# Transposing a gathered block by a DRAM round trip and VectorE's 32x32 blocks instead of on TensorE, in a routed MoE kernel

## The chip, the cores and the metric

The kernel runs on one core of a Trainium2 chip. The metric is the time on the device in microseconds (us), the median of several runs. The profile is one further execution, taken with the hardware profiler.

## The reference

Attention in chunks of 32 positions over 4 x 8 heads comes first; its output, 3072 tokens of 512 numbers, goes through a mixture of 8 experts, of which each token takes the one with the highest logit:

```
x = attn_out.transpose(0, 2, 1, 3).reshape(3072, 512)
logits = x @ w_gate + modality_bias[modality_id]
e_idx = argmax(logits, axis=1)
gate_w = softmax(logits)[arange(3072), e_idx]
for e in range(8):
    mask = e_idx == e
    h = maximum(x[mask] @ w1[e], 0)          # 512 -> 1024
    out[mask] = gate_w[mask, None] * (h @ w2[e])   # 1024 -> 512
```

All arrays are float32.

## The kernel before, in words

The first 160 us or so compute the attention and the routing. The attention output lies in DRAM as `xd`, one row of 512 numbers and the gate for each token; tables on the chip list for each expert its tokens.

The rest is a row of **slots**. A slot multiplies 256 tokens of one expert. `slot(row)` does three things at once: TensorE multiplies the tokens that the slot before prepared, the queues fetch the tokens and weights of `row`, and ScalarE and VectorE prepare them. The rows in this execution are 0 (in the first part of the program), 1, 2, 3, then 12 and 13 (`ROW_R1`, `ROW_X`), 14 to 17 (four of seven optional ones) and 33, 34; the last slot has no row to prepare. Eight optional short slots between 3 and 12 are skipped. The text calls the slot that prepares row 12 "slot 12".

A slot has two phases on TensorE. The first is `mm1(f)` for f = 0 to 7, 12 matmuls each: a product of float32 numbers is made of three products of rounded parts, the high part of w by the high and low part of x (`xth`, `xtl`), and the low part of w by the high part of x. The second is `mm2(f)`, 6 matmuls each. In the first phase ScalarE and VectorE finish h and split the eight blocks of w2 into parts (`conv(8 + f)`: a cast on ScalarE, a subtraction on VectorE). In the second they split the eight blocks of w1 of the next row (`conv(0)` to `conv(7)`, in `prepare(f)`), and TensorE transposes the next row's x: `trans(half)`, twice four 128x128 transposes into PSUM, from where ScalarE and VectorE take the two parts. Slots 3 and 12 also bring 32 extra tokens each (`gather_rest`, `trans_rest`), which the slot behind multiplies along.

SyncE (SP) issues the weight loads, in program order: w1 of a row at the head of its slot, w2 behind the first phase, eight transfers of 256 KB each. From row 1 on a load has a condition, which is false where the expert is that of the row before; then nothing is moved. GpSimd (POOL) issues the indirect transfers in its program order: the store of the results, then `keep` (it copies the lists and gates that the store and `finish` need later), then the gather of the next 256 tokens. SP, POOL, TensorE and, in this part, ScalarE and VectorE run in the order in which the program is written. Each optional slot is a branch on every engine; at the end of a skipped group the engines pass a join, where each one waits for its own work and then counts its semaphores on.

Of the kernel before, what the change touches and what calls it, by code (L numbers as in the profile page):

```python
# [20 lines left out]
P = 128  # L21
# [12 lines left out]
HEAD = 3  # L34
LAST = 3
# [17 lines left out]
def tile_chunk_attention_top1_moe(  # L53
# [31 lines left out]
    xd = dram.tile([N, XW], F32, name="xd")  # L85
    qf = q.rearrange("b h s d -> (b h s) d")
# [588 lines left out]
    w1h, w1l = [xa.tile([P, 8, 512], F32R, name=f"w1{i}") for i in range(2)]  # L675
    for f in range(8):
        raw[f] = xa.tile([P, 512], F32, name=f"raw{f}")
        wh[f], wl[f] = w1h[:, f], w1l[:, f]
    xp = hp = xg = xth = xtl = ix = gx = hh = hl = None
    ix_now = const.tile([P, 2], I32, name="ix_now")  # L680
    gate_now = const.tile([P, 2], F32, name="gate_now")
    ev = {}

    def load_w(row, half):
        if half == 0:
            if row == 0:
                ev[0] = nc.values_load(regs0[0:1, 0:1], engines=[mybir.EngineType.SP], min_val=0, max_val=E - 1,
                                       skip_runtime_bounds_check_because="the place of one of 8 experts")
            else:
                r = (regs1 if row < 2 else regs)[row:row + 1]  # L690
                ev[row] = nc.values_load(r[:, 0:1], engines=[mybir.EngineType.SP], min_val=0, max_val=E - 1,
                                         skip_runtime_bounds_check_because="the place of one of 8 experts, or 0")
                ev[row, "c"] = nc.values_load(r[:, 1:2], engines=[mybir.EngineType.SP], min_val=0, max_val=1,
                                              skip_runtime_bounds_check_because="a comparison gives 0 or 1")
        e = ev[row]
        kw = {} if row == 0 else {"cond": ev[row, "c"]}
        for f in range(8):
            if half == 0:
                nc.sync.dma_start(
                    raw[f].rearrange("p (c f) -> p c f", f=P),  # L700
                    w1[ds(e, 1), :, f * P:(f + 1) * P].rearrange("o (c p) f -> p (o c) f", p=P), **kw)
            else:
                nc.sync.dma_start(raw[8 + f], w2[ds(e, 1), f * P:(f + 1) * P, :].rearrange("o p d -> p (o d)"), **kw)
# [31 lines left out]

    def trans(half):
        t = bank().rearrange("p (c n) -> p c n", c=2)
        for cc in range(2):
            for tt in range(2):
                c = 2 * half + cc  # L740
                nc.tensor.transpose(t[:, cc, tt * P:(tt + 1) * P], xg[tt][:, c * P:(c + 1) * P], ident)  # L741
        sl = slice(2 * half, 2 * half + 2)
        nc.scalar.copy(xth[:, sl, 0:256], t)  # L743
        nc.vector.tensor_sub(xtl[:, sl, 0:256], t, xth[:, sl, 0:256].bitcast(F32))

    def trans_rest(i):
        t = bank()[:, 0:4 * NR].rearrange("p (c n) -> p c n", c=4)
        for c in range(4):
            nc.tensor.transpose(t[:, c], xgr[i][:, c * P:(c + 1) * P], ident[0:NR, 0:NR])
        nc.scalar.copy(xth[:, :, 256:], t)  # L750
        nc.vector.tensor_sub(xtl[:, :, 256:], t, xth[:, :, 256:].bitcast(F32))

    def mm1(f, rest=False):
# [36 lines left out]
    def finish(t):  # L790
        nc.scalar.activation(outs[t], pos[t], AF.Copy, scale=gate_now[:, t:t + 1])  # L791

    def store():
        put = [
            nc.gpsimd.indirect_dma_start(  # L795
                out=out, out_offset=bass.IndirectOffsetOnAxis(ap=ix_now[:, t:t + 1], axis=0), in_=outs[t], in_offset=None,
# [151 lines left out]
    gxr = hp.tile([NR, 1], I32, name="gxr")  # L948
    outs = [hp.tile([P, DM], F32, name=f"o{t}") for t in range(2)]
# [19 lines left out]
    def begin(row, opening=False):  # L969
        if row is not None:  # L970
            load_w(row, 0)
        if not opening:
            for t in range(2):
                finish(t)
            store()
        keep()
        if row is not None:
            gather(row)

    def prepare(f):  # L980
        for i in ((0, 1), (2, 3), (4,), (5,), (6, 7))[f] if f < 5 else ():
            conv(i)
        if f in (2, 3):
            trans(f - 2)

    def slot(row, rest=None, rest_next=None, opening=False):
        begin(row, opening)
        if rest_next is not None:
            gather_rest(rest_next)
        if not opening:  # L990
            for f in range(8):
                mm1(f, rest is not None)
                conv(8 + f)
        if rest is None and row is not None:
            load_w(row, 1)
        for f in range(6):
# [10 lines left out]
            elif row is not None:  # L1007
                prepare(f)
            if f == 3 and rest_next is not None:
                trans_rest(rest_next)  # L1010
        mm2(6, (0,))
        mm2(7, (0,))
        if row is None:
            finish(0)
# [9 lines left out]
        if row is None:  # L1024
            finish(1)
            store()
# [71 lines left out]
```

## Time and profile before

| | |
|---|---|
| median of 3 runs | 453.59 us (453.19 to 454.4) |
| profiled execution | 455.18 us, its span 453.4 us |
| TensorE matmul | 425.5 us busy, 94% of the span |
| VectorE | 310.5 us, 68% |
| ScalarE | 261.6 us, 58% |
| GpSimd | 195.8 us, 43% |
| DMA | 61.66 MB, mean 136 GB/s |

Busy time is what an engine's instructions took, and the share is that of the whole span, the attention part included. Matmuls overlap, so the start of one to the start of the next tells more than the duration of one.

### The profile page before, as it was taken

What the parts mean: (1) busy time and instruction counts of PE and PEld (TensorE: products, weight loads), DVE (VectorE), ACT (ScalarE), POOL (GpSimd) and SP (SyncE); (2) the same over time, 40 slices, a digit from 0 to 9 for tenths busy, and PEclk for the clock granted to TensorE, in tenths of its full rate; (3) what the DMA queues carried; (4) which work ended last, traced back from release to release, by engine and by line L of the source; (5) the groups of instructions that cost most, each with busy time, mean ns of one, the idle gap of its engine ahead of it and who ended that gap; (6) DMA issues with size and microseconds to landing.
All of it is one profiled execution on the core that took longest, in us unless ns stands there. A gap on an engine that the chain in (4) does not pass through costs nothing. (4 is left out here: it accounts for less than half of the span.)

```text
span 453.4 us, 11700 instructions
## 1 busy us (share of the span) xinstructions
PE 425.5 (94%) x4009; PEld 359.0 (79%) x4009; DVE 310.5 (68%) x746; ACT 261.6 (58%) x524; POOL 195.8 (43%) x373
## 2 busy tenths in 40 slices
PE   7879999999977998999999999999999999999993
PEld 4658787776856787989796977989898988898982
DVE  7888799797877699848465454757666574848430
ACT  5747776675636664747366455656565655657421
POOL 8867679579798932214051211303040404040201
PEclk9989999999979999999999999999999999999997
DMA  6899999999977502177196834202662201111101
GB/s 185 149 227 205 220 218 205 207 209 198 220 180 213 192 3 93 54 227 226 38 261 208 225 97 142 90 0 95 180 210 76 90 5 50 47 49 48 46 2 46
DMA packets 74818, 61.66 MB, mean 136 GB/s; under 512 B 36091, under 2 KB 64979, under 8 KB 74740
## 3 DMA queue, kind: packets, MB, share of 16 engines
q1 hardware_dynamic: 68000, 41.50, 40.2%
q0 software_dynamic: 5888, 19.11, 13.8%
q8 instruction: 36, 0.59, 0.6%
q14 instruction: 42, 0.34, 0.3%
q10 hardware_dynamic: 852, 0.11, 0.2%
HBM read 77.43 MB, written 12.76 MB: 199 GB/s over the span
## 5 line engine op out<-in xcount | busy, mean ns | idle before, releaser
L760 PEld LDWEIGHTS tr<-xt,w 128*128 128x128 f32 x1152 | 141.0, 189 | 4.9 <-issue 2.6
L760 PE MATMUL tr<-xt,w 128*128 128x256 f32 (+1 forms) x1152 | 142.9, 284 | 1.8 <-PEq L1059 0.6
L770 PE MATMUL av<-wh,h 128*128 128x512 f32 x384 | 128.4, 400 | 0.0
L795 POOL DMA_INDIRECT out_dram<-o,ix_now x24 | 24.2, 1008 | 157.1 <-ACT o L791 156.2
L764 DVE SCALAR_TENSOR_TENSOR h<-tr,h 128x256 fp32r<-128x256 f32 x96 | 40.6, 423 | 70.8 <-ACT h L761 53.1
L770 PEld LDWEIGHTS av<-wh,h 128*128 128x128 f32 x384 | 72.2, 188 | 17.3 <-issue 1.7
L770 PE MATMUL av<-wl,h 128*128 128x512 f32 x192 | 75.8, 395 | 0.0
L289 POOL COPY vw<-vw 24x384 f32<-24x384 f32 (+1 forms) x128 | 61.1, 515 | 24.5 <-DMA vw<-in_v_dram 23.2
L708 DVE TENSOR_TENSOR wl<-raw,wh 128x512 fp32r<-128x512 f32 x91 | 63.0, 692 | 8.1 <-ACT wh L706 0.8
L761 ACT ACTIVATE h<-tr 128x256 fp32r<-128x256 f32 x96 | 36.8, 385 | 51.8 <-PE tr L760 32.7
L708 DVE TENSOR_TENSOR w<-raw,w 128x512 fp32r<-128x512 f32 x93 | 60.4, 694 | 8.4 <-ACT w L706 8.4
L706 ACT CAST wh<-raw 128x512 fp32r<-128x512 f32 x96 | 58.8, 614 | 1.3 <-DMA raw<-in_moe_w_dram 1.3
L706 ACT CAST w<-raw 128x512 fp32r<-128x512 f32 x96 | 53.8, 622 | 0.0
L791 ACT ACTIVATE o<-av,gate_now 128x512 f32<-128x512 f32 x24 | 16.2, 689 | 46.3 <-PE av L770 37.3
L770 PEld LDWEIGHTS av<-wl,h 128*128 128x128 f32 x192 | 36.2, 188 | 7.1
L331 ACT COPY kbd<-tr 64x672 f32<-64x672 f32 x47 | 36.5, 777 | 6.4 <-PE tr L325 5.5
L369 PE MATMUL av<-vw,PT 128*32 128x130 f32 x768 | 29.3, 286 | 3.7 <-ACT PT L359 1.8
L359 ACT ACTIVATE PT<-tr 128x384 f32<-128x384 f32 x32 | 15.8, 492 | 28.6 <-PE tr L357 28.1
L339 PE MATMUL sc<-kbd,qT 128*32 128x128 f32 x768 | 29.3, 289 | 1.9 <-POOL kbd L313 1.9
L723 POOL DMA_INDIRECT xg<-xd,gx x24 | 26.5, 1105 | 9.8 <-POOL gx L721 6.2
L369 PEld LDWEIGHTS av<-vw,PT 128*32 128x32 f32 x768 | 20.5, 113 | 9.3 <-ACT PT L359 4.3
L743 ACT CAST xt<-tr 128x512 fp32r<-128x512 f32 x24 | 13.9, 586 | 23.0 <-PE tr L741 13.4
(237 smaller groups left out, 524.5 us busy)
## 6 DMA issues: line engine op xcount, KB each, us to landing
raw<-in_moe_w_dram SPq DMA_DIRECT2D x192, 256.0 KB
k<-in_k_dram SPq DMA_DIRECT2D x16, 384.0 KB
q<-in_q_dram SPq DMA_DIRECT2D x16, 384.0 KB
xd<-xb POOLq DMA_DIRECT2D x16, 384.0 KB, 6.0
vw<-in_v_dram SPq DMA_DIRECT2D x32, 184.0 KB
vw<-in_mem_v_dram SPq DMA_DIRECT2D x32, 48.0 KB
vw<-in_v_dram SPq DMA_DIRECT2D x32, 6.0 KB
vw<-in_v_dram SPq DMA_DIRECT2D x32, 2.0 KB
```

What stands on the lines that cost most here:

```text
L289: nc.gpsimd.tensor_copy(vw[r0:r0 + 24, c + 1:c + 1 + w, h, 0:D], vw[r0 + 32:r0 + 56, c:c + w, h, 0:D])
L331: copy(dst.rearrange("p c (i j) -> p c i j", j=2)[:, :, :, j], win)
L339: nc.tensor.matmul(sc[32 * j:32 * j + 32, t * P:(t + 1) * P], qT[:, 32 * c:32 * c + 32], kbd[:, c].rearrange("p h m -> p (h m)"), start=Tr ...
L369: nc.tensor.matmul(avb[32 * j:32 * j + 32, t * W:(t + 1) * W], PT[:, t * P + 32 * j:t * P + 32 * j + 32], vw[:, c].rearrange("p h d -> p ( ...
L706: nc.scalar.copy(wh[i], raw[i])
L708: (eng or nc.vector).tensor_sub(wl[i][:, s], raw[i][:, s], wh[i][:, s].bitcast(F32))
L723: nc.gpsimd.indirect_dma_start(out=xg[t], out_offset=None, in_=xd[0:rows], in_offset=bass.IndirectOffsetOnAxis(ap=gx[:, t:t + 1], axis=0))
L760: nc.tensor.matmul(pw, wt[f][:, c * P:(c + 1) * P], x[:, c, 0:w], start=(n == 0), stop=(n == 11))
L761: nc.scalar.activation(hh[:, f], ph, AF.Relu)
L764: nc.vector.scalar_tensor_tensor(hl[:, f], ph, 0.0, hh[:, f].bitcast(F32), op0=ALU.max, op1=ALU.subtract)
L770: nc.tensor.matmul(pos[t], x, w[8 + f], start=(f == 0 and n == 0), stop=(f == 7 and n == 2))
L795: nc.gpsimd.indirect_dma_start(out=out, out_offset=bass.IndirectOffsetOnAxis(ap=ix_now[:, t:t + 1], axis=0), in_=outs[t], in_offset=None, ...
```

## The change

From row 3 on (`NWHOLE` = 3) x is no longer transposed by TensorE. `send` copies the gathered rows to DRAM (`xs`, and `xsr` for the 32 extra tokens), and `fetch` reads them back as `xq`: partition 32a + s holds quarter a (128 of the 512 numbers) of the tokens s, 32 + s, 64 + s and so on. VectorE transposes 32x32 blocks of it (`turn`, and `turn_rest` for the extra tokens) into `xv`, and `turned` splits `xv` into its two parts as before. Rows of x then stand in another order over the partitions, so w1 is loaded in that order too: each of the eight transfers now fills 32 partitions with four pieces of 512 numbers (2 KB) where before each filled 128 partitions with four pieces of 128 (512 bytes), and a block of w1 is complete only when four transfers have landed. Row 3 loads w1 without a condition. Send and fetch stand in SP's order in front of the w1 load.

On POOL, `keep` and the gather now stand in front of the store, in every slot; the list and the gates that the store and `finish` still need are copied once more (`ix_out`, `gate_out`).

SP at the head of slot 3, before (`raw_2957` is the last block of w2 of row 2, `raw_188` and `raw_189` the first blocks of w1 of row 3):

```order
L703 DMA raw_2957<-in_moe_w_dram 128x512
L691 TENSOR_LOAD regs
L693 TENSOR_LOAD regs
L699 ISA
L699 DMA raw_188<-in_moe_w_dram 128x4x128
L699 ISA
L699 DMA raw_189<-in_moe_w_dram 128x4x128
```

The same place now (`raw_2955` is the last block of w2 of row 2, `raw` is w1):

```order
L713 DMA raw_2955<-in_moe_w_dram 128x512
L755 DMA xsr_85<-xgr_2958 32x512
L757 DMA xs<-xg_2709 128x512
L757 DMA xs<-xg_2710 128x512
L763 DMA xqr<-xsr_85 32x128
L764 DMA xq<-xs 32x8x128
...
L695 TENSOR_LOAD regs
L697 TENSOR_LOAD regs
L709 ISA
L709 DMA raw<-in_moe_w_dram 32x4x512
```

Three sends and eight fetches (four pairs) stand between the last w2 block and the first w1 transfer; in slots without extra tokens there are two sends and four fetches.

VectorE in the second phase of slot 3, before (`w` is the low part of w1, `xt` that of x):

```order
L708 TENSOR_TENSOR w_187<-raw_191,w_186 128x512
L708 TENSOR_TENSOR w_187<-raw_192,w_186 128x512
L744 TENSOR_TENSOR xt_2714<-tr,xt_2713 128x2x256
L708 TENSOR_TENSOR w_187<-raw_193,w_186 128x512
L744 TENSOR_TENSOR xt_2714<-tr,xt_2713 128x2x256
L751 TENSOR_TENSOR xt_2714<-tr,xt_2713 128x4x32
L708 TENSOR_TENSOR w_187<-raw_194,w_186 128x512
L708 TENSOR_TENSOR w_187<-raw_195,w_186 128x512
L1053 TENSOR_LOAD nsl x2
L1059 COMPARE_AND_BRANCH
```

And now:

```order
L718 TENSOR_TENSOR w_190<-raw,w_189 128x512 x4
L767 STREAM_TRANSPOSE xv<-xq 128x4x4x32
L718 TENSOR_TENSOR w_190<-raw,w_189 128x512
L767 STREAM_TRANSPOSE xv<-xq 128x4x4x32
L718 TENSOR_TENSOR w_190<-raw,w_189 128x512
L751 TENSOR_TENSOR xt_2712<-xv,xt_2711 128x2x256
L784 STREAM_TRANSPOSE xvr<-xqr 128x128
L751 TENSOR_TENSOR xt_2712<-xvr,xt_2711 128x4x32
L718 TENSOR_TENSOR w_190<-raw,w_189 128x512 x2
L751 TENSOR_TENSOR xt_2712<-xv,xt_2711 128x2x256
L1100 TENSOR_LOAD nsl x2
L1106 COMPARE_AND_BRANCH
```

The second split of x is now VectorE's last instruction ahead of the branch, and x no longer comes out of PSUM.

POOL at the head of slot 3, before (`out_dram` is the store, `xg` the gather):

```order
L795 DMA out_dram<-o_2965,ix_now 3072x512
L795 DMA out_dram<-o_2966,ix_now 3072x512
L711 COPY ix_now<-ix 128x2
L713 COPY gate_now<-xg_2711 128x1
...
L723 DMA xg_2711<-xd,gx 128x516
L723 DMA xg_2712<-xd,gx 128x516
...
L733 DMA xgr_2960<-xd,gxr 32x516
```

And now:

```order
L722 COPY ix_193<-ix_192 128x2
L723 COPY gate_195<-gate_194 128x2
L724 COPY ix_192<-ix 128x2
L726 COPY gate_194<-xg_2709 128x1
...
L736 DMA xg_2709<-xd,gx 128x516
L736 DMA xg_2710<-xd,gx 128x516
...
L746 DMA xgr_2958<-xd,gxr 32x516
L830 DMA out_dram<-o_2967,ix_193 3072x512
L830 DMA out_dram<-o_2968,ix_193 3072x512
```

The store has moved from the head of the list to its end.

The diff, cut:

```diff
+NWHOLE = 3
...
+    xs = dram.tile([2 * P, DM], F32, name="xs")
+    xsr = [dram.tile([NR, DM], F32, name=f"xsr{i}") for i in range(2)]
...
+    raw1 = xa.tile([P, 8, 512], F32, name="raw")
     for f in range(8):
-        raw[f] = xa.tile([P, 512], F32, name=f"raw{f}")
+        raw[f] = raw1[:, f]
...
-        kw = {} if row == 0 else {"cond": ev[row, "c"]}
+        kw = {} if row == 0 or row == NWHOLE and half == 0 else {"cond": ev[row, "c"]}
         for f in range(8):
-            if half == 0:
+            if half == 0 and row < NWHOLE:
                 nc.sync.dma_start(
                     raw[f].rearrange("p (c f) -> p c f", f=P),
                     w1[ds(e, 1), :, f * P:(f + 1) * P].rearrange("o (c p) f -> p (o c) f", p=P), **kw)
+            elif half == 0:
+                src = w1[ds(e, 1), :, (f // 4) * DM:(f // 4 + 1) * DM]
+                c = f % 4
+                nc.sync.dma_start(
+                    raw1[32 * c:32 * c + 32, f - c:f - c + 4],
+                    src[:, c * P:(c + 1) * P].rearrange("o (c s) f -> s (o c) f", s=32), **kw)
...
-    def keep():
+    def keep(opening):
+        if not opening:
+            nc.gpsimd.tensor_copy(ix_out, ix_now)
+            nc.gpsimd.tensor_copy(gate_out, gate_now)
         nc.gpsimd.tensor_copy(ix_now, ix)
...
+    def split(x, sl, cols):
+        nc.scalar.copy(xth[:, sl, cols], x)
+        nc.vector.tensor_sub(xtl[:, sl, cols], x, xth[:, sl, cols].bitcast(F32))
+
+    def send(rest):
+        if rest is not None:
+            nc.sync.dma_start(xsr[rest], xgr[rest][:, 0:DM])
+        for t in range(2):
+            nc.sync.dma_start(xs[t * P:(t + 1) * P], xg[t][:, 0:DM])
+
+    def fetch(rest):
+        for a in range(4):
+            sl = slice(32 * a, 32 * a + 32)
+            if rest is not None:
+                nc.sync.dma_start(xqr[sl], xsr[rest][:, a * P:(a + 1) * P])
+            nc.sync.dma_start(xq[sl], xs[:, a * P:(a + 1) * P].rearrange("(j s) d -> s j d", s=32))
+
+    def turn(half):
+        nc.vector.transpose(
+            xv.rearrange("p c (t j s) -> p t j c s", t=2, j=4)[:, half],
+            xq[:, 4 * half:4 * half + 4].rearrange("p j (c s) -> p j c s", c=4))
+
+    def turned(half):
+        sl = slice(2 * half, 2 * half + 2)
+        split(xv[:, sl], sl, slice(0, 256))
...
-    def mm1(f, rest=False):
+    def mm1(f, rest=False, whole=True):
...
-            nc.tensor.matmul(pw, wt[f][:, c * P:(c + 1) * P], x[:, c, 0:w], start=(n == 0), stop=(n == 11))
+            i, j = (f, c) if whole else (f - f % 4 + c, f % 4)
+            nc.tensor.matmul(pw, wt[i][:, j * P:(j + 1) * P], x[:, c, 0:w], start=(n == 0), stop=(n == 11))
...
-    def begin(row, opening=False):
+    def begin(row, opening=False, rest_next=None):
+        if row is not None and row < NWHOLE:
+            load_w(row, 0)
+        keep(opening)
         if row is not None:
-            load_w(row, 0)
+            gather(row)
+            if rest_next is not None:
+                gather_rest(rest_next)
+            if row >= NWHOLE:
+                send(rest_next)
+                fetch(rest_next)
+                load_w(row, 0)
         if not opening:
             for t in range(2):
-                finish(t)
-            store()
-        keep()
-        if row is not None:
-            gather(row)
+                finish(t, gate_out)
+            store(ix_out)
-
-    def prepare(f):
+    def prepare(f, whole=False):
+        if f in (2, 3) and not whole:
+            turn(f - 2)
         for i in ((0, 1), (2, 3), (4,), (5,), (6, 7))[f] if f < 5 else ():
             conv(i)
-        if f in (2, 3):
+        if f in (2, 3) and whole:
             trans(f - 2)
+        if f in (3, 4) and not whole:
+            turned(f - 3)
```

## Rows read from the trace of the kernel before

**Rows 1.** Busy time by stretch: us, each engine's busy us, clock, DMA share, GB/s.
```profile
340.00:344.00 4.00, 4.00 (x20) 3.22 (x19) 3.70 (x7) 3.50 (x7) 0.00 (x0) 1.00 0.67 209
348.00:352.00 4.00, 4.00 (x19) 3.22 (x18) 1.23 (x3) 1.04 (x2) 0.02 (x1) 1.00 0.00 0
```

**Rows 2.** Chain of waits in order of time: start us, us, what.
```profile
387.80 4.20 PE av L770 x18
392.00 0.44 PE tr L741 x4
...
399.87 11.36 PE tr L760 x96
```

**Rows 3.** Groups of instructions from 200 us: busy us, mean ns, idle before.
```profile
L744 DVE TENSOR_TENSOR xt<-tr,xt 128x512 fp32r<-128x512 f32 x18 | 12.4, 691 | 8.2 <-ACT xt L743 8.2
L741 PE MATMUL tr<-ident,xg 128*128 128x128 f32 x72 | 10.9, 273 | 0.0
```

**Rows 4.** Timeline of TensorE in slot 12: start us, us, instruction.
```profile
247.20 0.60 PE L741 MATMUL tr<-ident,xg 128*128 128x128 f32 x4
...
248.43 0.39 PE L770 MATMUL av<-wl,h 128*128 128x512 f32 x1
```

**Rows 5.** Timelines of TensorE (slot 2) and SP (slots 3 and 12).
```profile
194.39 0.60 PE L741 MATMUL tr<-ident,xg 128*128 128x128 f32 x4
...
191.33 6.73 SPq L699 DMA_DIRECT2D raw<-in_moe_w_dram  x8
224.70 7.55 SPq L699 DMA_DIRECT2D raw<-in_moe_w_dram  x8
```

**Rows 6.** Timeline of GpSimd in slot 12.
```profile
232.07 0.19 POOL L711 COPY ix_now<-ix 128x2 int32<-128x2 int32 x1 [3.64 <-DMA out_dram<-o,ix_now]
...
233.90 1.06 POOL L723 DMA_INDIRECT xg<-xd,gx  x1 [0.28 <-POOL gx L721]
...
237.37 0.97 POOL L733 DMA_INDIRECT xgr<-xd,gxr  x1 [0.28 <-POOL gxr L732]
```

**Rows 7.** DMA issues: the last number is us from issue to landing.
```profile
xg<-xd,gx POOLq DMA_INDIRECT x24, 3.7
out_dram<-o,ix_now POOLq DMA_INDIRECT x24, 2.7
xgr<-xd,gxr POOLq DMA_INDIRECT x2, 3.1
```

**Rows 8.** Busy time by stretch: loads of w2 with gathers, then of w1.
```profile
208.00:212.00 4.00, 4.00 (x35) 3.97 (x34) 3.18 (x6) 2.42 (x7) 2.56 (x4) 1.00 0.90 310
...
321.00:329.00 8.00, 8.00 (x42) 6.63 (x41) 3.64 (x6) 3.44 (x7) 0.45 (x1) 1.00 0.96 259
```

**Rows 9.** Timeline of VectorE in slot 3, second phase.
```profile
213.51 3.10 DVE L708 TENSOR_TENSOR w<-raw,w 128x512 fp32r<-128x512 f32 x5
...
219.88 1.29 DVE L708 TENSOR_TENSOR w<-raw,w 128x512 fp32r<-128x512 f32 x2
```

**Rows 10.** Line L1059, the skipped branch: ns min/median/max, first and last start us.
```profile
L1059 ACTq COMPARE_BRANCH  x1: 55/55/55, 219.9 to 219.9; - x1
...
L1059 DVEq COMPARE_BRANCH  x1: 72/72/72, 221.3 to 221.3; - x1
L1059 ACTq EVENT_SEMAPHORE  x1: 17/17/17, 222.3 to 222.3; - x1
L1059 DVEq EVENT_SEMAPHORE  x1: 21/21/21, 224.5 to 224.5; - x1
```

**Rows 11.** Timeline of TensorE: the first phases of slots 12 and 13.
```profile
225.17 13.02 PE L760 MATMUL tr<-xt,w 128*128 128x288 f32 x96 [0.61 <-PEq L1059]
...
253.79 12.95 PE L760 MATMUL tr<-xt,w 128*128 128x288 f32 x96
```

**Rows 12.** Busy time by stretch before the first slots.
```profile
126.00:129.00 3.00, 1.14 (x9) 0.80 (x8) 2.87 (x13) 1.46 (x4) 2.85 (x6) 1.00 0.54 129
...
132.00:138.00 6.00, 6.00 (x75) 4.90 (x79) 2.10 (x5) 0.97 (x2) 5.03 (x12) 0.50 1.04 282
```

More of the change, by code (lines that the diff above doesn't have):

```diff
@@ L675, in tile_chunk_attention_top1_moe @@
     w1h, w1l = [xa.tile([P, 8, 512], F32R, name=f"w1{i}") for i in range(2)]
+    raw1 = xa.tile([P, 8, 512], F32, name="raw")
     for f in range(8):
-        raw[f] = xa.tile([P, 512], F32, name=f"raw{f}")
+        raw[f] = raw1[:, f]
         wh[f], wl[f] = w1h[:, f], w1l[:, f]
     xp = hp = xg = xth = xtl = ix = gx = hh = hl = None
-    ix_now = const.tile([P, 2], I32, name="ix_now")
-    gate_now = const.tile([P, 2], F32, name="gate_now")
+    ix_now, ix_out = [const.tile([P, 2], I32, name=f"ix_{i}") for i in range(2)]
+    gate_now, gate_out = [const.tile([P, 2], F32, name=f"gate_{i}") for i in range(2)]
     ev = {}
@@ L741, in trans, with turn_rest @@
                 nc.tensor.transpose(t[:, cc, tt * P:(tt + 1) * P], xg[tt][:, c * P:(c + 1) * P], ident)
[L742 to L751, printed above, removed]
-    def mm1(f, rest=False):
+        split(t, slice(2 * half, 2 * half + 2), slice(0, 256))
+    def turn_rest():
+        nc.vector.transpose(xvr, xqr.rearrange("p (c s) -> p c s", c=4))
+        split(xvr, slice(0, 4), slice(256, 256 + NR))
+    def mm1(f, rest=False, whole=True):
         w = 256 + (NR if rest else 0)
@@ L788, in fold_rest, with finish, store @@
             bounds_check=N - 1, oob_is_err=False)
-    def finish(t):
-        nc.scalar.activation(outs[t], pos[t], AF.Copy, scale=gate_now[:, t:t + 1])
-    def store():
+    def finish(t, gate):
+        nc.scalar.activation(outs[t], pos[t], AF.Copy, scale=gate[:, t:t + 1])
+    def store(to):
         put = [
             nc.gpsimd.indirect_dma_start(
-                out=out, out_offset=bass.IndirectOffsetOnAxis(ap=ix_now[:, t:t + 1], axis=0), in_=outs[t], in_offset=None,
+                out=out, out_offset=bass.IndirectOffsetOnAxis(ap=to[:, t:t + 1], axis=0), in_=outs[t], in_offset=None,
                 bounds_check=N - 1, oob_is_err=False)
@@ L806, in tail_mm1 @@
         for c in range(4):
-            wsl = [w[:, 4 * half:4 * half + 4, c * P:(c + 1) * P] for w in (w1h, w1l)]
+            wsl = [w[:, 4 * half + c] for w in (w1h, w1l)]
             for x, w in ((xth, wsl[0]), (xtl, wsl[0]), (xth, wsl[1])):
@@ L948, in tile_chunk_attention_top1_moe @@
     gxr = hp.tile([NR, 1], I32, name="gxr")
+    xq = hp.tile([P, 8, P], F32, name="xq")
+    xqr = hp.tile([P, P], F32, name="xqr")
+    xv = hp.tile([P, 4, 256], F32, name="xv")
+    xvr = hp.tile([P, 4, NR], F32, name="xvr")
     outs = [hp.tile([P, DM], F32, name=f"o{t}") for t in range(2)]
@@ L967, in tile_chunk_attention_top1_moe @@
     pump(99, True)
-    def begin(row, opening=False):
+    def begin(row, opening=False, rest_next=None):
+        if row is not None and row < NWHOLE:
+            load_w(row, 0)
+        keep(opening)
         if row is not None:
-            load_w(row, 0)
+            gather(row)
[5 more added lines that the diff above has]
+                load_w(row, 0)
         if not opening:
             for t in range(2):
-                finish(t)
-            store()
-        keep()
-        if row is not None:
-            gather(row)
-    def prepare(f):
+                finish(t, gate_out)
[3 more added lines that the diff above has]
+            turn(f - 2)
         for i in ((0, 1), (2, 3), (4,), (5,), (6, 7))[f] if f < 5 else ():
             conv(i)
-        if f in (2, 3):
+        if f in (2, 3) and whole:
             trans(f - 2)
+        if f in (3, 4) and not whole:
+            turned(f - 3)
     def slot(row, rest=None, rest_next=None, opening=False):
-        begin(row, opening)
-        if rest_next is not None:
-            gather_rest(rest_next)
+        begin(row, opening, rest_next)
         if not opening:
             for f in range(8):
-                mm1(f, rest is not None)
+                mm1(f, rest is not None, row is not None and row <= NWHOLE)
                 conv(8 + f)
@@ L1007, in slot @@
             elif row is not None:
-                prepare(f)
+                prepare(f, row < NWHOLE)
             if f == 3 and rest_next is not None:
-                trans_rest(rest_next)
+                turn_rest()
         mm2(6, (0,))
@@ L1013, in slot @@
         if row is None:
-            finish(0)
+            finish(0, gate_now)
         if opening:
@@ L1024, in slot @@
         if row is None:
-            finish(1)
-            store()
+            finish(1, gate_now)
+            store(ix_now)
     def short_slot(row):
```

## The prediction

> **What bounds the kernel now.** I read the busy times by stretch first, then the chain of waits, then the timelines of the single engines at the places that the change touches. From about 176 us on TensorE never rests: in every stretch of four microseconds it is busy throughout at the full clock, while VectorE and ScalarE swing between 1 and 3.7 us of the four [rows 1]. The chain of waits is TensorE's own program almost alone: 96 matmuls of the first layer in 11.4 to 11.6 us, then 48 of the second at 0.233 us each (4.20 / 18), with two pieces of four transposes between them, 0.44 us apiece [rows 2]. So a matmul taken out of a slot is time won, as long as the next slot's first matmul has its operands when TensorE comes to it. That is the question: before, they were always there but at one place, the join behind the skipped short slots, where TensorE idled 0.61 us [rows 11].
>
> **What goes.** From 200 us on there are 72 of the 96 x transposes [rows 3], eight in each of nine slots (rows 3, 12 to 17, 33, 34). Two pieces of 0.44 are 0.88 us a slot, 7.9 us in nine. In slots 3 and 12 (the first with 32 extra tokens) four small transposes follow the second piece: from 247.20 to 248.43 are 1.23 us for both pieces and one matmul of 0.23, so the small ones cost 1.23 - 0.23 - 0.44 = 0.56 [rows 2, 4], twice 1.1. **At most 9.0 us are to be won.**
>
> **What comes, on VectorE.** Two transposes of 128x512 a slot, an operation that no row shows. The nearest is the subtraction of the same size at 0.69 us [rows 3]; I take 0.65. Below, half of that is the bound; above, what VectorE can carry: its last subtraction of the first phase is out at 213.5, 1.7 us behind TensorE's own change of phase, and then it has eight conversions at 0.62 [rows 9], two splits of x and the two transposes, 1.7 + 5.0 + 1.3 + 2T, before a second phase of 48 x 0.233 = 11.2 us is over. That fits up to T = 1.6. It no longer waits for TensorE's x there, so at T = 0.65 it ends sooner than it must: nothing on the path in the seven slots 13 to 17, 33 and 34.
>
> **What comes, on the queues.** A slot's x goes out to DRAM and back, 1 MB more traffic, and SP issues it in front of the w1 load. In a slot in the middle of a run this is hidden: the gather now stands ahead of the store on GpSimd, so the send runs early; the fetch waits only for VectorE's second transpose of the slot before, some 5 us into a second phase, and w1 is needed a whole slot later. In slots 14, 15, 17, 33 and 34 no w1 is moved (their conditions are false: in the stretch before slot 17's end the DMA engines move nothing [rows 1]). Cover is missing at two places, one behind the other.
>
> Slot 3. Row 2's x is still transposed by TensorE, until 194.99, and gather 3 overwrites the same tile, so it cannot start before 195.3 [rows 5]. The third gather starts 3.5 us behind the first [rows 6], 198.8, and lands 3.1 later, 201.9. A send has no row; the store of as many bytes lands in 2.7 us [rows 7], which gives 204.6; I give the first fetch 2.7 too, 207.3, as the first w1 quarter waits for it (eight completion counters go round SP's transfers). Before, w1 left at 191.3 [rows 5]; it leaves 16 us later.
>
> How long the new w1 load takes, L, is the unknown that decides. Its 2.1 MB took 8.1 us at 259 GB/s in 512-byte pieces; 2 KB pieces (w2 among them) ran at 310, which makes 6.8 [rows 8]. Each new transfer fills only 32 partitions, which no row shows at this size; were it half as fast as the old, L would be 16. I take 9.5, near the row of the same load but behind it, and 0.7 for the first byte: the second half is there at 217.5.
>
> [...]
>
> Then VectorE has a cast to wait for (0.6), four conversions, a transpose, two splits (seven at 0.62 to 0.69) and the small rest (0.5): 5.7 us, so 223.2. Behind that stands the skipped branch: at the same point before, VectorE's branch came at 221.3 and its semaphore at 224.5, 3.2 us [rows 10], and slot 12's first matmul waits for it. So it starts at 226.6 instead of 225.17 [rows 11]: TensorE, ready 1.44 us sooner, waits about 2.9.
>
> Slot 12. Here all stands behind the join. GpSimd's keep waits for ScalarE's semaphore, 2.4 us behind its branch [rows 10], about 224.9; the third gather starts 5.3 us later [rows 6], plus 0.4 for two more copies, 230.6; landing 3.1, send 2.7, fetch 2.7: w1 leaves at 239.1 (224.7 before [rows 5]) and its second half lands at 249.3. VectorE ends at 255.0, ScalarE's part of x 0.3 sooner. TensorE needs 253.79 - 225.17 = 28.6 us for the slot [rows 11], less 1.44: ready at 253.8, it goes on at 254.9. That is 1.1 us later than before, although 2.9 us of work are gone.
>
> From slot 13 on w1 has time again: it leaves behind w2 and the fetch at about 262, and its first half is wanted at 268. Seven slots win 0.88 each, 6.2 us. **Sum: -6.2 + 1.1 = -5.1 us.** The profiled execution took 455.18 us for a span of 453.4; the median of the runs is 453.59. Taken from the median that is **448.5 us**. The order of the stores, the two copies on GpSimd and the wait of finish for them I cost at nothing: the stores feed no one before the next finish, a slot later.
>
> **The rivals.** *All hidden.* If L is 6.8, as the larger pieces in the rows suggest, slot 12 stalls hardly at all; but VectorE's own list in slot 3 still ends at 213.5 + 5.0 + 1.3 + 1.3 + 0.5 = 221.6, and 3.2 later TensorE has lost 1.1. That makes -9.0 + 1.1 = -7.9, 445.7 us. For it: larger pieces ran faster, 310 against 259 GB/s [rows 8]. Against it: each transfer fills only a quarter of the partitions. Chance 0.15 (445 to 447).
>
> *Slow quarters.* Each microsecond more of L is paid twice, once in slot 3, whose end moves slot 12's gathers, and again in slot 12. At 11 the sum is -2.1, 451.5 us; at 12 the gain is gone. Chance 0.15 (451 to 455). [...]
>
> *VectorE becomes the bound (slower).* If a 32x32 transpose of 4-byte elements takes T over 1.6 us, every slot's x comes late, by 2 x (T - 1.6), and the two joins lose two more transposes each, 4 x (T - 0.65). At T = 1.7 that is 7 x (0.2 - 0.88) + 1.1 + 4.2 = +0.5: from there the whole is slower. At T = 2.1 it is 0.8 + 1.1 + 5.8 = +7.7, 461 us. For it: no row has the operation. Against: 512 elements a partition, and everything else of this size takes 0.69. On the same side lies L beyond 12.6, and a fall of the clock behind the two stalls: where TensorE had been busy 1.14 of 3 us the granted clock afterwards stood at 0.50, the lower of its two levels, for six [rows 12]. That would cost up to 3 us at either join; the stalls that I forecast are single ones of 1 to 3 us. Chance together 0.18.
>
> **How the numbers follow.** The forecast, L from 8 to 10.5, holds 0.52 and reaches from 447 to 451. A difference under 0.3% (1.4 us: 452.2 to 455.0) can't be told from none. Faster: 0.52 + 0.15 and a small part of the slow quarters, 0.70; the same 0.12; slower 0.18. The range that leaves out two in ten reaches into the fast case and to the far end of the slow quarters: 445 to 455.
>
> **What would show it right or wrong.** Right: 24 TensorE transposes of x left, seven slots 0.88 us shorter without a gap between them; slot 12's first matmul 2 to 4 us behind the last of slot 3, ended by VectorE; slot 13's first about 1 us late, ended by ScalarE or VectorE behind a w1 load that leaves near 239. The transposes should read 0.6 to 0.7 us. Wrong: gaps at the head of slots 14 to 17, w1 in 7 us or in 12, or slot 12's gathers running before the join is passed.

## The result, and the profile after

The changed kernel takes **460.25 us** (459.61 to 461.15) where the kernel before takes 453.59 (453.19 to 454.4): a ratio of 1.0133, 95% interval 1.0095 to 1.0171. It is slower by 6.7 us; 448.5 was forecast, and the range ended at 455. The profiled execution took 461.15 us, its span is 459.4.

The first phases on TensorE in the changed kernel, slots 3, 12, 13, 14 and 15 (start us, us, instruction, in brackets the idle time before it and what ended it; compare [rows 11]):

```profile
200.44 11.38 PE L795 MATMUL tr<-xt,w 128*128 128x256 f32 x96
...
230.73 1.33 PE L795 MATMUL tr<-xt,w 128*128 128x288 f32 x4 [7.71 <-ACTq L1106]
...
233.12 14.56 PE L795 MATMUL tr<-xt,w 128*128 128x288 f32 x92 [1.06 <-DVEq L1106]
...
263.29 0.53 PE L795 MATMUL tr<-xt,w 128*128 128x288 f32 x2 [1.20 <-ACT xt L750]
264.85 14.31 PE L795 MATMUL tr<-xt,w 128*128 128x288 f32 x94 [1.03 <-ACT xt L750]
...
293.41 11.56 PE L795 MATMUL tr<-xt,w 128*128 128x256 f32 x96
316.01 11.37 PE L795 MATMUL tr<-xt,w 128*128 128x256 f32 x96
```

And of the kernel before, slots 3, 14 and 15:

```profile
200.42 11.52 PE L760 MATMUL tr<-xt,w 128*128 128x256 f32 x96
...
281.79 11.52 PE L760 MATMUL tr<-xt,w 128*128 128x256 f32 x96
305.22 11.52 PE L760 MATMUL tr<-xt,w 128*128 128x256 f32 x96
```

Both enter slot 3 at the same time. From slot 14 on the change does what it says: 22.60 us from the first phase of slot 14 to that of slot 15 instead of 23.43, without a wait between them, and 166.0 us from slot 14 to the end of the span instead of 171.6. (Behind slot 17, where the optional slots that are left are skipped, both kernels have one more wait of 0.55 us, at 376.20 before and 383.97 now; the prediction, which speaks of one place only, overlooked it.) Everything is lost in between, in what I call **the stretch**, from slot 3's first matmul to slot 14's: 92.97 us instead of 81.37. Its sum: waits of 7.71 + 1.06 + 1.20 + 1.03 = 11.0 instead of 0.61; slot 12's first phase 15.9 us instead of 13.02 and slot 13's 14.8 instead of 12.95, 4.8 more; less 3.8 for the transposes that are gone from slots 3, 12 and 13. That is +11.4 of the 11.6.

What the first wait is made of stands on SP and ScalarE. SP in slots 3 and 12, shortened (compare [rows 5]):

```profile
201.89 0.34 SPq L755 DMA_DIRECT2D xsr<-xgr  x1
...
206.12 0.33 SPq L764 DMA_DIRECT2D xq<-xs  x1
...
210.24 4.14 SPq L709 DMA_DIRECT2D raw<-in_moe_w_dram  x8
...
238.52 0.34 SPq L755 DMA_DIRECT2D xsr<-xgr  x1
...
242.78 0.33 SPq L764 DMA_DIRECT2D xq<-xs  x1
...
247.00 4.75 SPq L709 DMA_DIRECT2D raw<-in_moe_w_dram  x8
```

ScalarE's conversions of w1 there (blocks 0 to 3, then 4 and 5):

```profile
218.42 2.18 ACT L716 CAST w<-raw 128x512 fp32r<-128x512 f32 x4 [5.67 <-DMA raw<-in_moe_w_dram]
223.56 1.14 ACT L716 CAST w<-raw 128x512 fp32r<-128x512 f32 x2 [2.96 <-DMA raw<-in_moe_w_dram]
...
259.28 1.14 ACT L716 CAST w<-raw 128x512 fp32r<-128x512 f32 x2 [2.16 <-DMA raw<-in_moe_w_dram]
```

The first half of w1 is used 8.2 us after w1 left, the second 13.3 (slot 3) and 12.3 (slot 12). Busy time by stretch (columns as in [rows 1]):

```profile
212.00:222.00 10.00, 10.00 (x45) 8.01 (x44) 4.11 (x8) 2.93 (x6) 0.00 (x0) 1.00 1.07 216
...
214.00:219.00 5.00, 5.00 (x23) 4.03 (x22) 0.00 (x0) 0.58 (x2) 0.00 (x0) 1.00 1.07 210
...
223.00:224.00 1.00, 0.02 (x1) 0.00 (x0) 0.00 (x0) 0.44 (x1) 0.00 (x0) 1.00 1.05 385
...
228.00:231.00 3.00, 0.27 (x1) 0.27 (x2) 1.90 (x3) 1.06 (x3) 0.26 (x3) 0.50 0.04 12
...
234.00:242.00 8.00, 8.00 (x49) 8.00 (x49) 3.53 (x7) 3.62 (x12) 4.41 (x6) 0.77 0.64 209
...
266.00:272.00 6.00, 6.00 (x39) 6.00 (x38) 2.47 (x5) 2.70 (x9) 1.69 (x2) 0.80 0.60 215
```

In the first two it is w1 that moves: the DMA engines are full (share 1.07) and still pass no more than 210 to 216 GB/s, in all 2.16 MB in ten microseconds, and w1 has 2.1. SP issues w2 behind it, from 214.73 on; the rate rises only at 222, to 385 GB/s, and w2's transfers, also of 256 KB in pieces of 2 KB, each fill 128 partitions. In the others the granted clock is down at 0.50, the lower of the two levels that stand in this trace (the other is 1.00; what lies between is a mean over both), in and behind the idle 7.7 us, and comes back between 234 and 242; in slot 13's first phase it reads 0.80 once more. The branch itself (compare [rows 10]; duration, then start):

```profile
L1106 PEldq COMPARE_BRANCH  x1: 7405/7405/7405, 219.7 to 219.7; - x1
...
L1106 ACTq COMPARE_BRANCH  x1: 55/55/55, 228.1 to 228.1; - x1
L1106 DVEq COMPARE_BRANCH  x1: 72/72/72, 230.1 to 230.1; - x1
L1106 ACTq EVENT_SEMAPHORE  x1: 17/17/17, 230.7 to 230.7; - x1
L1106 DVEq EVENT_SEMAPHORE  x1: 21/21/21, 233.0 to 233.0; - x1
```

ScalarE and VectorE come to it 8 to 9 us later than before, and TensorE waits for both: its first four matmuls start at 230.73 behind ScalarE's semaphore, the other 92 at 233.12 behind VectorE's.

### The profile page after: what moved, and what is told of

Same layout as the page of the kernel before. It is cut to its first block, busy times and chain, and to the rows that moved or that the text cites. A ratio compares the mean times of both kernels' runs of the same rounds, so it can differ in the third digit from the quotient of the medians.

```text
span 459.4 us, 11667 instructions
## 1 busy us (share of the span) xinstructions
PE 420.3 (91%) x3929; PEld 354.1 (77%) x3929; DVE 322.7 (70%) x766; ACT 261.6 (57%) x524; POOL 200.9 (44%) x395
## 5 line engine op out<-in xcount | busy, mean ns | idle before, releaser
L795 PE MATMUL tr<-xt,w 128*128 128x256 f32 (+1 forms) x1152 | 148.3, 290 | 12.1 <-ACTq L1106 7.7
L795 PEld LDWEIGHTS tr<-xt,w 128*128 128x128 f32 x1152 | 145.7, 194 | 15.9 <-ACTq L1106 8.2
L805 PE MATMUL av<-wh,h 128*128 128x512 f32 x384 | 124.5, 397 | 0.0
L830 POOL DMA_INDIRECT out_dram<-o,ix x24 | 24.3, 1011 | 87.8 <-ACT o L826 83.9
L826 ACT ACTIVATE o<-av,gate 128x512 f32<-128x512 f32 x24 | 16.1, 688 | 31.6 <-PE av L805 26.5
L342 PE MATMUL sc<-kbd,qT 128*32 128x128 f32 x768 | 28.2, 281 | 2.3 <-POOL kbd L316 2.3
L372 PEld LDWEIGHTS av<-vw,PT 128*32 128x32 f32 x768 | 19.7, 109 | 10.1 <-ACT PT L362 4.5
L342 PEld LDWEIGHTS sc<-kbd,qT 128*32 128x32 f32 x768 | 19.8, 111 | 7.5 <-issue 4.2
```

What stands on the lines that cost most here:

```text
L342: nc.tensor.matmul(sc[32 * j:32 * j + 32, t * P:(t + 1) * P], qT[:, 32 * c:32 * c + 32], kbd[:, c].rearrange("p h m -> p (h m)"), start=Tr ...
L372: nc.tensor.matmul(avb[32 * j:32 * j + 32, t * W:(t + 1) * W], PT[:, t * P + 32 * j:t * P + 32 * j + 32], vw[:, c].rearrange("p h d -> p ( ...
L795: nc.tensor.matmul(pw, wt[i][:, j * P:(j + 1) * P], x[:, c, 0:w], start=(n == 0), stop=(n == 11))
L805: nc.tensor.matmul(pos[t], x, w[8 + f], start=(f == 0 and n == 0), stop=(f == 7 and n == 2))
L830: nc.gpsimd.indirect_dma_start(out=out, out_offset=bass.IndirectOffsetOnAxis(ap=to[:, t:t + 1], axis=0), in_=outs[t], in_offset=None, boun ...
```

## The experiments

**Theory A:** w1 is late in slots 3 and 12, where nothing covers it, because it stands behind the round trip on SP and because the transfers to 32 partitions run slowly (210 to 216 GB/s against 385 for w2); the clock's fall comes on top. Rivals: one of these alone; the round trip itself; the transposes; GpSimd's new order. Between profiled executions the start of slot 3 varies from 199.7 to 204.6 us, though little is changed ahead of it (only GpSimd's order); and the kernel before, which was timed again beside each series, took from 453.59 to 457.50 us. So I compare the stretch and the waits of one trace, and take the ratio to the kernel before in the same series for the whole. Waits are those of TensorE in the stretch.

| kernel | waits | stretch | slot 14 to end | ratio to before (95%) |
|---|---|---|---|---|
| before | 0.6 | 81.37 | 171.6 | 1 |
| changed | 11.0 | 92.97 | 166.0 | 1.0133 (1.0095 to 1.0171) |
| 1 w1 first | 4.0 | 83.40 | 166.0 | 0.9964 (0.9920 to 1.0008) |
| 3 spin | 10.1 | 94.14 | 165.7 | 1.0204 (1.0143 to 1.0265) |
| 4 GpSimd only | 0.8 | 81.55 | 170.8 | 1.0011 (0.9989 to 1.0033) |
| 5 w1 first, one fetch | 3.5 | 82.37 | 166.0 | 0.9919 (0.9879 to 0.9960) |
| 6 128 partitions | 4.7 | 84.43 | 166.0 | 0.9953 (0.9911 to 0.9995) |
| 7 all three | 2.9 | 81.76 | 166.0 | 0.9859 (0.9803 to 0.9915) |
| 8 one fetch | 10.7 | 92.47 | 166.1 | 1.0107 (1.0037 to 1.0177) |
| 9 all three, from slot 12 | 0.5 | 78.96 | 167.1 | 0.9840 (0.9795 to 0.9885) |
| 10 w1 first, from slot 12 | 1.5 | 80.23 | 167.2 | 0.9906 (0.9871 to 0.9941) |
| 11 from slot 12 | 6.6 | 88.58 | 168.8 | 1.0046 (1.0010 to 1.0083) |
| 12 the same with spin | 2.9 | 86.42 | 166.0 | 0.9987 (0.9956 to 1.0018) |

In 9 to 11 the time from slot 14 to the end holds a wait of 1.8 to 2.2 us behind slot 17, where the other runs have 0.55 to 1.1. Some of it (0.6 to 1.6 us) is time in which TensorE waited for nothing that the profile shows; why is open.

**1. The first half of w1 in front.**

```diff
-        if row is not None and row < NWHOLE:
+        if row is not None:
             load_w(row, 0)
...
                 fetch(rest_next)
-                load_w(row, 0)
```

> Rows from the fourth on load the first half of w1 at the head of the slot again, in front of send and fetch; all else as in the changed kernel. Theory A (the lost time is the late start of w1 behind ten small transfers on SP, with half-rate quarters and the clock's fall on top): w1 leaves about 199 instead of 210.24, the first conversions wait for no DMA, slot 12's first phase starts at 225 to 227.5 instead of 230.73, slot 13's without its 2.2 us stall and at full clock; with the 9.0 us saved in the nine slots, 445 to 449 us. Theory B (the quarters' slow rate alone is it, wherever w1 stands): over 453. Theory C (the round trip by DRAM itself is late, w1 is only in front of it): now the fetch lies behind 2 MB of w1 and the transposes wait, 452 or more.

The stretch loses 9.6 of its 11.6 us. By the time alone (454.70 us, before 454.82) theories B and C would fit; the stretch puts B out: with a head start the quarters' rate costs little. But 2.64 us of wait at the branch and 1.4 in slot 13 remain, as theory C had it: the fetch lies behind w1 now (the first quarter of x leaves at 210.84, 10.2 us into the slot), and ScalarE waits for the first transpose:

```profile
219.29 0.62 ACT L750 CAST xt<-xv 128x512 fp32r<-128x512 f32 x1 [3.27 <-DVE xv L767]
```

And behind the wait of 2.64 us the clock falls here too. TensorE's first phase of slot 12 takes 14.8 us instead of 13.0 (the second row is the stretch of time, clock 0.52):

```profile
225.82 14.83 PE L795 MATMUL tr<-xt,w 128*128 128x288 f32 x96 [2.64 <-ACTq L1105]
```

```profile
226.00:229.00 3.00, 2.92 (x12) 2.58 (x13) 0.00 (x0) 1.26 (x2) 1.84 (x7) 0.52 0.11 20
```

The forecast 445 to 449 was too low; the time can't be told from before's.

**2 and 6. The quarters.** In the second experiment each transfer brings one chunk to all 128 partitions; its source has the four row groups of 128 outermost.

```diff
-                nc.sync.dma_start(
-                    raw1[32 * c:32 * c + 32, f - c:f - c + 4],
-                    src[:, c * P:(c + 1) * P].rearrange("o (c s) f -> s (o c) f", s=32), **kw)
+                nc.sync.dma_start(raw[f], src.rearrange("o (a c s) f -> c (o a) s f", c=4, s=32)[f % 4], **kw)
```

> w1 stays behind send and fetch, but each of its eight transfers carries one chunk to all 128 partitions (2-KB rows, as w2's) instead of four chunks to 32 partitions: the same layout in SBUF, and a conversion waits for one transfer instead of four. Theory A: w1 leaves at 210 as before, but moves at about 320 GB/s instead of 210 to 217; first conversion starts at about 213.5 instead of 218.4, the last is ready about 219 instead of 223.6; the stall at the join shrinks from 7.7 to 3.5 to 5 us and slot 13's goes; 450 to 454 us. Theory B (slow quarters alone): 447 or less. If the rate of the quarters costs nothing (only the place on SP counts): 458 to 460.

It took 509 us, a ratio of 1.1198 (1.1136 to 1.1260), and answers another question. While w1 moves in slot 3:

```profile
214.00:219.00 5.00, 5.00 (x24) 3.98 (x23) 1.72 (x3) 1.10 (x2) 0.00 (x0) 1.00 0.27 97
```

A DMA share of 0.27 is what four of the 16 engines give when they alone are busy (0.27 x 16 = 4.3). The outermost extent of the transfer's source is 4 here, where it is 32 in the changed kernel, with a share of 1.07. That the extent decides how many engines take part was my guess from these two rows. So the sixth experiment puts 128 rows outermost, by letting partition p hold rows 4p to 4p + 3 of w1:

```diff
+                nc.sync.dma_start(raw[f], src.rearrange("o (p c) f -> c p (o f)", c=4)[f % 4], **kw)
...
-            xq[:, 4 * half:4 * half + 4].rearrange("p j (c s) -> p j c s", c=4))
+            xq[:, 4 * half:4 * half + 4].rearrange("p j (s c) -> p j c s", c=4))
```

> The second experiment again in a form whose outermost extent is 128 rows, so that all 16 DMA engines can share it: partition p holds rows 4p to 4p+3 of w1, each of eight transfers brings one chunk to all 128 partitions in 2-KB rows, and VectorE's transposes read every fourth column. w1 stays behind send and fetch. Theory A: w1 leaves at 210 as in the changed kernel and moves at about 320 GB/s; first conversion at about 213.5 instead of 218.4; stall at the join 3.5 to 5 us, none in slot 13, less fall of the clock; 450 to 455 us. If the rate of the quarters costs nothing: 459 to 461. Theory B (slow quarters alone): 447 or less.

The same stretch of time, w1 alone again (SP issues w2 from 218.63 on):

```profile
214.00:219.00 5.00, 5.00 (x24) 4.05 (x23) 3.60 (x6) 2.76 (x5) 0.00 (x0) 1.00 0.91 293
```

293 GB/s at a share of 0.91, where the second experiment had 97 at 0.27 and the changed kernel 210 at 1.07. So the guess held for 128 rows. w1 leaves as late as in the changed kernel (9.7 us into slot 3 instead of 9.8), yet ScalarE's first conversion (at 215.45, w1 having left at 212.61) runs 2.8 us behind it instead of 8.2, the wait at the branch is 4.7 instead of 8.8 us, and slot 13's is gone. Theory A holds as to the rate; the time, 455.26 us, lies just above its 450 to 455 in a series in which the kernel before took 457.50. The experiment changes two things at once: a conversion now also waits for one transfer instead of four. How the two share the gain wasn't tried.

**3. Matmuls of zeros in the waits**, to take away the clock's fall.

```diff
+            for _ in range({ROW_R1: 14, ROW_X: 9}.get(row, 0)):
+                nc.tensor.matmul(bank(), idle[:, 0:P], idle[:, P:640], start=True, stop=True)
```

> The changed kernel with 14 matmuls of zeros in front of slot 12's first phase and 9 in front of slot 13's, about 0.22 us each, in the time in which TensorE waits anyway; nothing else differs. Theory A: the waits stay as long, but the clock does not fall to 0.50 and 0.80, so the first phases of slots 12 and 13 take 12.9 to 13.5 us instead of 15.9 and 14.8: 455.5 to 457.5 us. Theory D (the fall of the clock is the main loss, the waits a small one): under 454. Theory E (the stretched phases are no matter of the clock but of late operands): 460, as the changed kernel.

The time missed, 465.04 us; the trace shows why (TensorE, slots 12 and 13):

```profile
235.19 0.58 PE L1039 MATMUL tr<-idle 128*128 128x512 bf16 x1 [8.00 <-ACTq L1108]
237.86 4.71 PE L1039 MATMUL tr<-idle 128*128 128x512 bf16 x13 [2.09 <-DVEq L1108]
242.22 13.14 PE L795 MATMUL tr<-xt,w 128*128 128x288 f32 x96
...
269.62 2.12 PE L1039 MATMUL tr<-idle 128*128 128x512 bf16 x9
271.45 13.06 PE L795 MATMUL tr<-xt,w 128*128 128x288 f32 x96
```

Behind the branch the zero matmuls wait like the others, the first for ScalarE and the rest for VectorE; so 13 of the 14 came on top of the wait. As to the clock theory A holds: both first phases take 13.1 us. In slot 13 the nine fill the wait as meant: from slot 12's last matmul to the end of slot 13's first phase are 14.7 us instead of 17.1. In the stretch this leaves 1.2 us more than in the changed kernel; in the profiled execution slot 3 also starts 4.2 us later although nothing is changed ahead of it, and why is open.

**4. Only GpSimd's new order**, on the kernel before: indices and gates kept in a second pair of tiles, keep and gathers in front of the store.

> The kernel before with nothing but the new order on GpSimd: the indices and gates are kept in a second pair of tiles, and keep and the gathers stand in front of finish and store. Theory A: GpSimd waits in slots 12 and 13 as before for what follows, the gathers start at most some us sooner, and nothing on TensorE's path hangs on them: 453.6, within 1.4 us. Theory F (the gathers, moved in front of the store, delay the stores or the gate of the row, and so slots): 455 or more.

The same time, 455.69 us where before took 454.82, as theory A has it. Theory F is out.

**5 and 8. Fewer transfers for the round trip.** The scratch is laid out so that a fetch is one transfer.

```diff
+            nc.sync.dma_start(xs[t].rearrange("a p d -> p a d"), xg[t][:, 0:DM].rearrange("p (a d) -> p a d", a=4))
...
+        nc.sync.dma_start(
+            xq.rearrange("p (t j) d -> p t (j d)", t=2), xs.rearrange("t a (s j) d -> (a s) t (j d)", j=4))
```

> The first experiment (first half of w1 at the head of the slot) with the round trip in fewer transfers: the scratch is laid out as [quarter, token, 128], so send is one transfer a token tile with 512-byte rows and fetch is one transfer for the rows and one for the rest rows, instead of eight. Theory A (what was left over in the first experiment, 2.6 us at the join and 1.4 us in slot 13, is the fetch's eight issues of 0.33 to 0.45 us and their landings): first VectorE transpose of slot 3 four to five us sooner, no stall at the join beyond before's 0.6, none in slot 13; 446 to 450 us where before takes 454.8. Theory C (the round trip is late by its two DRAM latencies, not by its issues): as the first experiment, 451 to 456.

> The changed kernel with the one-fetch layout of the scratch alone; w1 stays behind it and keeps its 32-partition quarters. Theory A: fetch's SP time falls from 3.3 to under 1 us, w1 leaves about 207.3 as the prediction had it instead of 210.24; stall at the join 7.7 to about 4.7 us, slot 13's gone, part of the clock's fall too: 452 to 456 us. Theory C' (the landing of the round trip, not its issues, holds w1): 458 to 461.

Alone (8) it gains 0.5 us in the stretch, and theory A's 452 to 456 fails (461.40 us, before 457.50). SP and ScalarE in slot 3 of the eighth experiment:

```profile
207.21 4.12 SPq L709 DMA_DIRECT2D raw<-in_moe_w_dram  x8
```

```profile
222.57 1.14 ACT L716 CAST w<-raw 128x512 fp32r<-128x512 f32 x2 [4.06 <-DMA raw<-in_moe_w_dram]
```

Counted from slot 3's first matmul (199.75 there), w1 leaves 2.3 us sooner, but its second half is used at 22.8 instead of 23.1. So the issues on SP do hold back w1's leaving, but not its use; where the 2 us go between the issue and the landing the rows don't settle. With w1 in front (5) the same layout brings 1.0 us; slot 13's wait goes, the branch keeps 3.5, and theory A fails there too: the first transpose stands 16.5 us into slot 3 instead of 16.7, where it had four to five us sooner, and the time is 452.73 us (before 457.50) instead of 446 to 450. The layout has a price as well (row of 5):

```profile
L766 DVE STREAM_TRANSPOSE xv<-xq 128x512 f32<-128x512 f32 x18 | 19.7, 1097 | 1.1 <-DMA xq<-xs 1.1
```

The transposes write every fourth element there and take 1.10 us instead of 0.70.

**7. All three mends.**

> All three together: w1 at the head of the slot, the scratch laid out for one fetch, and w1's transfers over 128 partitions. Theory A: with w1 at the head its rate no longer matters, so no more than 1 us under the run with the first two alone: 445 to 449 us, every slot from the fourth on 0.88 us shorter and no stall left but those before had. Theory B (slow quarters matter even there, since they hold the rings while the gathers run): 2 us or more under that run.

A ratio of 0.9859; the stretch is 0.6 us under the fifth experiment's, as theory A has it (the ratios lie further apart, 0.6%, but their intervals overlap). The time, 450.05 us (before 457.50), lies above its 445 to 449, and against it the branch keeps 2.9 us of wait, and slot 12's first phase is 14.8 us instead of 13.0:

```profile
226.28 0.80 PE L791 MATMUL tr<-xt,w 128*128 128x288 f32 x4 [0.95 <-ACTq L1101]
229.05 14.03 PE L791 MATMUL tr<-xt,w 128*128 128x288 f32 x92 [1.98 <-DVEq L1101]
```

**9, 10 and 11. Not before slot 12.** Rows up to 11 and the first rest rows stay with TensorE's transposes:

```diff
-NWHOLE = 3
+NWHOLE = 12
...
-                turn_rest()
+                if row < NWHOLE:
+                    trans_rest(rest_next)
+                else:
+                    turn_rest()
```

> The kernel with all three mends (w1 at the head of the slot, one fetch, w1 over 128 partitions), but the way by the scratch begins at slot 12 instead of slot 3: row 3 and the first rest rows are turned on TensorE as before, so no VectorE transposes stand ahead of the taken branch. Theory A (what the three mends left over, 2.9 us of wait and 1.9 us of a slowed first phase in slot 12, comes from VectorE's 11 us of in-order work ahead of the branch): slot 12's first phase begins as before's, its clock stays full, slot 13 has no stall; from the start of slot 3's first phase to slot 14's 79 to 80 us (before 81.4, the three mends 81.8), the whole 1.4 to 2.0 per cent under before, about 2 us under the run with the three mends. Rival G (the branch's wait comes from the transfers and the instruction fetch under their load, w1 or no w1): slot 12's wait stays 2 to 3 us.

> As the run beside it, with only w1 at the head of the slot: eight fetches and the 32-partition quarters stay. Theory A: no wait at the branch; slot 13 keeps a stall of up to 1.5 us, since there the fetch's eight issues lie behind the third gather; 79.5 to 82 us from slot 3's first phase to slot 14's, 1.0 to 1.8 per cent under before. If quarters or issues matter in every slot: no better than the first experiment, within 0.5 per cent of before.

> The changed kernel as it is (send and fetch in front of w1, eight fetches, quarters), beginning only at slot 12. Theory A: the wait at the branch (8.8 us in the changed kernel) and slot 12's slowed phase go, and slot 13's stall remains as far as w1's quarters land late behind the third gather: 1 to 3 us and a slowed phase of 1 to 2; 447 to 452 us where before takes 453.6, against 460 of the changed kernel, so that most of what was lost was lost at the one slot whose work must be done ahead of the branch. Rival H (every slot with late quarters loses the same): 456 or more.

With the three mends (9):

```profile
200.70 11.38 PE L797 MATMUL tr<-xt,w 128*128 128x256 f32 x96
225.21 13.02 PE L797 MATMUL tr<-xt,w 128*128 128x288 f32 x96 [0.50 <-PEq L1110]
252.48 12.94 PE L797 MATMUL tr<-xt,w 128*128 128x288 f32 x96
279.66 11.56 PE L797 MATMUL tr<-xt,w 128*128 128x256 f32 x96
```

The wait at the branch is before's, every phase runs at full speed, slots 12 and 13 are 27.2 to 27.3 us long. This experiment alone would leave rival G some room, since here the transfers too are gone from the time of the branch. But they had gone already in the seventh experiment, which still waited 2.9 us; its DMA engines from 220 to 226 (the column after the clock):

```profile
220.00:226.00 6.00, 5.33 (x23) 3.93 (x21) 4.55 (x8) 2.49 (x5) 0.00 (x0) 1.00 0.02 6
```

So rival G is out. This kernel has the lowest ratio of the study, 1.6% under before (448.72 us where before took 455.72); by the whole time it can't be told from the seventh experiment's, since their intervals overlap, but its stretch is 2.8 us shorter. With w1 in front alone (10) it is 0.9%, just short of the 1.0 to 1.8 expected, with 0.75 us of wait left in slot 13.

Without any mend (11) theory A's 447 to 452 is wrong, and rival H comes nearer: 457.93 us where before took 455.72.

```profile
226.54 13.02 PE L801 MATMUL tr<-xt,w 128*128 128x288 f32 x96 [0.64 <-PEq L1115]
259.18 0.85 PE L801 MATMUL tr<-xt,w 128*128 128x288 f32 x2 [5.21 <-ACT xt L750]
260.74 15.49 PE L801 MATMUL tr<-xt,w 128*128 128x288 f32 x94 [0.71 <-ACT xt L750]
```

The branch is clean, and the loss turns up one slot on. From slot 12's first matmul to slot 13's are 32.6 us here and 32.6 in the changed kernel (28.6 before): this is the length of slot 12's own path, from the gathers behind the branch by the round trip to the late w1. In the changed kernel 2.9 us of it were covered by TensorE's slow phase.

**12. The eleventh with 22 zero matmuls** in front of slot 13's first phase, where no branch holds them up.

> The run before with the way by the scratch from slot 12 on and w1 behind it, where slot 13's first phase waits 5.2 and 0.7 us behind no branch and then runs 16.3 instead of 12.95 us; now with 22 matmuls of zeros of about 0.22 us in that wait. Theory A (the longer phase is the granted clock's fall after the idle 5 us): the end of the wait stays where it is, the clock of that stretch stays 1.00 and the phase takes 13.0 to 13.5 us; from slot 3's first phase to slot 14's 85 to 86 us instead of 88.6, some 3 us off the whole. Theory E (the phase is slow because its operands or their reads are): still 16 us, 88.6 or more.

```profile
251.37 4.92 PE L1045 MATMUL tr<-idle 128*128 128x512 bf16 x22
257.51 0.53 PE L801 MATMUL tr<-xt,w 128*128 128x288 f32 x2 [1.22 <-ACT xt L750]
259.07 12.80 PE L801 MATMUL tr<-xt,w 128*128 128x288 f32 x94 [1.03 <-ACT xt L750]
```

Granted clock (the column before the DMA share) in the eleventh, then in the twelfth:

```profile
260.00:264.00 4.00, 3.29 (x14) 3.26 (x14) 1.57 (x3) 2.25 (x7) 2.02 (x2) 0.50 0.77 283
```

```profile
260.00:264.00 4.00, 4.00 (x32) 4.00 (x32) 2.17 (x4) 2.14 (x7) 1.90 (x2) 1.00 0.73 267
```

The phase takes 13.3 instead of 16.3 us, the clock stays at 1.00, the stretch 86.4 instead of 88.6 (a little over the 85 to 86 expected, the wait ending 0.5 later), and the whole goes from 1.0046 to 0.9987 times before. So theory E is out: the long first phase behind this wait is the clock's fall, 3 us after an idle time of 5 to 6.

## Why the prediction was wrong

**Right.** What is removed: 0.88 us a slot (0.83 measured from slot 14 to 15), 5.6 us from slot 14 on. The transposes: 0.65 assumed, 0.70 measured. VectorE hides them in every later slot. GpSimd's order costs nothing that can be told (experiment 4, a ratio of 1.0011). The two places, slots 3 and 12, the order of the events there, and the release of slot 12 by ScalarE and VectorE behind the branch are as forecast.

**Wrong: the size of L**, "I take 9.5, near the row of the same load". With 0.7 for the first byte the second half was to be used 10.2 us after w1 left; it was 13.3 and 12.3. In the prediction's terms L was 12.6 and 11.6, the far end of the rival "slow quarters", given 0.15. The row of the same load [rows 8] was for 128 partitions; measured are 210 GB/s to 32 partitions against 293 to 128 (experiment 6) and 385 for w2 in the same trace. But the rate is the smaller part of the miss: 2.1 MB at 210 GB/s are 10.0 us, 0.5 more than 9.5. The rest in slot 3 lies at its ends: the DMA engines are full only from 212 on (share 0.60 in the microsecond before), 1.8 us after w1 left, where the 0.7 had no row, and the cast starts 1.6 us after the rate of w1 ends at 222.

**Wrong: when w1 leaves.** The send was given 2.7 us, and the first fetch 2.7 until w1 may follow. From the first send to the first xq transfer are 4.2 us in slot 3 and 4.3 in slot 12, and from there to w1's first 4.1 and 4.2. So w1 left slot 3 at 210.24 instead of 207.3, and with the gathers behind the branch 16.3 us after slot 12's first matmul instead of 12.5. The reason given, that w1 waits for the first fetch, is not what the trace shows: between the last fetch and w1 SP waits only 0.2 us, for VectorE; what stands there is the issuing of the fetches. With one fetch (experiment 8) w1 leaves 2.3 us sooner, though that alone brings 0.5 us. Experiment 1 shows what the place in the queue is worth: in front of the round trip w1 gives back 9.6 of the 11.6 us.

**Wrong: the clock**, costed at nothing in the forecast and "up to 3 us at either join" only in a rival, although [rows 12] showed the fall. It took 2.9 and 1.9 us. Waits as short as the forecast ones would not have spared it: in experiment 1 a wait of 2.64 us, where 2.9 was forecast, is followed by a phase that is 1.8 us longer at a granted clock of 0.52. Experiment 12 shows the cause for the longer wait. Behind the 1.22 and 1.03 us that are left there the clock stays at 1.00, where behind 1.20 and 1.03 in the changed kernel it reads 0.80; why these two differ is open.

These three are the term "slot 13 starts 1.1 us late", which measured 9.5, with 1.0 of a second wait and 1.9 of the slowed phase behind it: 12.4. Together with the -6.4 won behind it this is the +6.0 of the span. The statement that each microsecond of L is paid twice is too simple: the clock's fall comes on top of the wait (2.9 us in slot 12), but the slow phase then hides a part of the next slot's lateness (those 2.9 us, experiment 11).

## What to carry to other kernels

Where an operation is moved to an idle engine by way of a DRAM round trip, look first at what queues behind the transfers, and let the large load that nobody holds up go in front of the small ones that wait. Price a load by its shape as well as its bytes (here 210 GB/s into 32 partitions and 293 into 128), from its issue to its first use, and give a new path a slot of its own to fill before a branch or a barrier comes that waits for every engine. If a forecast contains an idle TensorE of several microseconds, the fall of its clock belongs in the sum: here a phase of 13 us took 1.8 to 3.4 us more behind waits of 2.6 to 8.8 us.

## What the runs showed of the hardware beside that

VectorE's 32x32 transpose of float32, 128x512, takes 0.70 us with unit steps and 1.09 to 1.13 us if it reads or writes with a step of four elements (experiments 5 to 7). TensorE's branch took longer in the traces in which transfers ran beside it: 7.4 us in the changed kernel (the row above; DMA share 1.03 to 1.07 from 219 to 227), 5.3 us in the first experiment (0.73 from 220 to 225), and 3.5 us in the ninth, where they moved next to nothing at that time (0.01 to 0.05). That the transfers are the cause wasn't tried.

```profile
L1110 PEldq COMPARE_BRANCH  x1: 3507/3507/3507, 221.4 to 221.4; - x1
```

In the changed kernel it ended nothing, since ScalarE and VectorE were later still; in the ninth experiment the 0.50 us of wait at the branch end with TensorE's own sequencer.
